# Ten resident units instead of six ahead of each block's first tile in the fourth layer of a four-layer forward and backward pass

## The chip, the cores and the metric

The kernel runs on one core of one Trainium2 chip. The metric is the device time of one execution in microseconds, the median of several runs. TensorE is called PE (its weight loads PEld), VectorE DVE, ScalarE ACT, GpSimd POOL and SyncE SP.

## What is computed

A decode step of four layers and its gradients. The layers alternate between attention over a window of a key/value cache and an MLP with a Mish activation, and both kinds use the same weights twice:

```python
x = x + _A_ref(_layernorm(x), A_k_cache, A_v_cache, A_wq, A_wo)   # layer 1
x = x + _B_ref(_layernorm(x), B_w1, B_b1, B_w2)                   # layer 2
x = x + _A_ref(_layernorm(x), A_k_cache, A_v_cache, A_wq, A_wo)   # layer 3
x = x + _B_ref(_layernorm(x), B_w1, B_b1, B_w2)                   # layer 4
```

x has one row of 1024. Attention has 32 query heads and 4 key/value heads of 128, caches of 32768 positions of which the last 4096 are used, wq of 1024 x 4096 and wo of 4096 x 1024. The MLP has w1 of 1024 x 3584 and w2 of 3584 x 1024. All is bfloat16. Outputs are x and the gradients of x, both caches (4 x 32768 x 128 each), wq, wo, w1, b1 and w2. The caches' gradients are zero outside the window of 4096, so most of the bytes that the kernel writes are zeros.

## The kernel before

Every matrix product has a single row of x on one side, so each weight is read once by PE per use, and the weights have to be on the chip in two orientations: one for the forward product, the other for the backward one. The kernel keeps wq, K, V and wo in SBUF and turns them in place. A *unit* is a piece of 128 x 1024 of one of them; turning it is eight PE transposes of 128 x 128 into a PSUM tile `tp` (lines L258 and L282) and one copy back by ACT (L231) or DVE (L229). Units wait in a list sorted by the tensor's rank (wo, V, K, wq), and `fill(n)` turns the next n at the place in the program where it stands. `fill_kind(kind)` turns all that are left up to that kind, directly ahead of the product that needs them. Three PSUM tiles are shared by everything named `tp`, `op` or `dhp`.

The fourth layer (`mlp_B4`) needs w1 in both orientations. It works in four blocks of w1's columns: three of 1024 and one of 512. A block is loaded as four tiles of 512 KB (the last block as two) into the four buffers of ring `r4`, which lie in the K tensor, so that a block takes all of them. Per block come, in this order: `fwd` (for each tile first `fill(FT4[b][i])`, then the tile's matmuls), `fill(FB4[b][0])`, a selection and the Mish, `turn` (the tile's own transposes), `fill(FB4[b][1])`, `bwd`, and the release of the buffers by `rel`. `rel` calls `pump`, which issues the next loads in the queue (L182 for weights, L190 for K) as far as buffers are free. Then `zeros(ZB4[b])` issues that many transfers of zeros of 512 KB to the caches' gradients (L151, or L149 once the source is the smaller one).

All these transfers stand in SP's one queue in program order. A load whose buffer is not free holds up what stands behind it, and a transfer is held back until the eighth before it has landed.

Behind the fourth layer come the backward passes: layer 3 (`attn_bwd`, with its own lists of fills and zeros, `F_` and `Z_`; its last product `R<-wq` comes after `fill_kind("wq")`), layer 2 (`mlp_B2_bwd`: 14 tiles of w2 through `w2_pass`, then 16 of w1; six buffers of ring `rb` at first, which come free when layer 3 has used K), and layer 1. From there on `run_jobs` makes the weights' gradients as outer products (matmuls with two rows, copied out by `ev_out` at L890 on DVE and L893 on ACT) and writes them out (L965, L978, L996, L1001, L1097). The last zeros are issued among the first of these jobs: the third entry of `add("w2", ...)` says how many.

Of the kernel before, what the change touches and what calls it, by code (L numbers as in the profile page):

```python
# [21 lines left out]
def kernel(  # L22
# [65 lines left out]
    sB, sA, zlo, zt = misc[:, 0:1024], misc[:, 1024:2048], misc[:, 2048:3072], misc[:, 1024:3072]  # L88
# [654 lines left out]
    def attn_bwd(g_col, g_bf, l, sv, last, nxt, F_, Z_, step):  # L743
        fill_kind("wo")
        big = two_banks()
        for d in range(TD):
            for n in range(8):
                mm(big[n // 4][32 * (n % 4):32 * (n % 4) + 32, :].rearrange("p (h x) -> p h x", h=4),
                   bc(g_bf[:, d:d + 1]), wo[:, 4 * n:4 * n + 4, d * P:(d + 1) * P], d == 0, d == TD - 1, tile_position=(0, 32 * (n % 4)))
        if last:  # L750
            p_t, ds_t = sB, wo[:, 1, :]
            wo_dead()
            nc.gpsimd.dma_start(wo[:, 0, :], p3_d[:])
        else:
            p_t, ds_t = sv["p"], sA
        zeros(Z_[0])
        acc = one_tile("acc", HQ)
        j_cols(big, acc, 8, F_[0], True)
        do32 = wk("do32", HQ)
        nc.vector.tensor_copy(pad[:, :, 0:8], acc[:].rearrange("p (g h) -> p g h", g=G))  # L760
        nc.vector.tensor_copy(do32[:], acc[:])
        pr = jkf[:, 0:P]
        nc.vector.tensor_mul(pr[:].rearrange("p (c h) -> p c h", c=NC), do32[:, None, :].to_broadcast([P, NC, HQ]),
                             sv["o32"][:, None, :].to_broadcast([P, NC, HQ]))
        nc.gpsimd.tensor_copy(dos[:, LI[l], :], do32[:])
        step(0)
        fill(F_[1])
        fill_kind("V")
        big = two_banks()
        scores(big, Vf, False)  # L770
        sps = sm_tile(P, 1)
        mm(sps[:], pr[:], one[:], True, True)
        sd = wk("sd", 1)
        nc.vector.tensor_copy(sd[:], sps[:])
        zeros(Z_[1])
        for h in range(2):
            nc.vector.scalar_tensor_tensor(out=ds_t[:, h * 512:(h + 1) * 512], in0=big[h][:], scalar=sd[:, 0:1],
                                           in1=p_t[:, h * 512:(h + 1) * 512], op0=ALU.subtract, op1=ALU.mult)
        sv["p"], sv["ds"] = p_t, ds_t
        if not last:  # L780
            nc.gpsimd.dma_start(p3_d[:], sB)
            nc.gpsimd.dma_start(sB, p1_d[:])
            sv["p"] = wo[:, 0, :]
        step(1)
        fill(F_[2])
        to_keys(ds_t)
        fill_kind("K")
        qacc = one_tile("acc", HQ)
        step(2)
        keys_mm(K[:], fold, qacc, F_[3])  # L790
        if not last:
            rings["rb"] += range(2, 8)
            pump()
        nc.scalar.activation(dqpair[:, LI[l], :], qacc[:], ACT.Copy, scale=scale)
        zeros(Z_[2])
        step(3)
        fill_kind("wq")
        R = one_tile("R", 512)
        for h in range(HQ):
            for hf in range(2):  # L800
                g = 2 * hf + h % 2
                mm(R[32 * g:32 * g + 32, :].rearrange("p (t d) -> p t d", t=4), bc(dqpair[:, LI[l], h:h + 1]),
                   wq[:, 4 * hf:4 * hf + 4, h * P:(h + 1) * P], h < 2, h >= HQ - 2, tile_position=(0, 32 * g))
            if h % 4 == 3 and h < 31:
                step(4)
        y = d_cols(R, hook=lambda: step(5))
        tt = wk("xx", 2 * TD)
        nc.vector.tensor_copy(tt[:, 0:TD], y[:])
        return ln_bwd(tt, sv, g_col, nxt, hook=lambda: step(6))
# [62 lines left out]
    row_sp = {k: wo2[1 + i].rearrange("p (s x) -> p s x", s=2) for i, k in enumerate(("w2", "w1", "wo", "wq"))}  # L872
# [96 lines left out]
    def pair_half(R, c0, out_v, lhs_of, i):  # L969
        cs = [c0, c0 + 1]  # L970
        if i == 0:
            held_st[c0] = {c: stage() for c in cs}
        sts = held_st[c0]
        quad(R, [(*lhs_of(c, tt), slice(i * 512, (i + 1) * 512), sts[c][:, tt * 1024 + i * 512:tt * 1024 + (i + 1) * 512])
                 for c in cs for tt in range(2)])
        if i == 1:
            for c in cs:
                nc.sync.dma_start(out_v[c], sts[c].rearrange("p (t d) -> p t d", t=2))  # L978
# [45 lines left out]
    w2_out = out_8.rearrange("(c p t) d -> c p t d", p=P, t=2)  # L1024
# [3 lines left out]
    def wo_dead():  # L1028
        for sp in spreads:
            nc.gpsimd.memset(sp, 0.0)  # L1030
        w2_sp.append(rows_spread(apair, "blocks"))
        w2_sp.append(rows_spread(gpair[:, 2:4, :], "rep"))

        def rows(name, side, src, how):
            return lambda: rows_spread(src, how), lambda got: rows_turn(row_sp[name], side, got, how)

        def lay(out, src, k):
            return lambda: row_spread(src, k), lambda got: out.append(row_layout(got, k))

        def small_add():  # L1040
            db1 = kt([P, 2, NW2], BF16, "db1")
            nc.vector.tensor_add(db1[:], dh_l[0][:].rearrange("p (c t) -> p t c", t=2), dh_l[1][:].rearrange("p (c t) -> p t c", t=2))
            return db1

        def small(db1):
            col_out(x4_bf_l[0][:], TD, out_0[0, 0, :], 4)
            col_out(g0_l[0], TD, out_1[0, 0, :], 5)
            db_row = kp[0:NW2, 0:2, :].rearrange("c t x -> c (t x)").rearrange("c (p t) -> c p t", t=2)
            for t in range(2):
                dbps = ptile()  # L1050
                nc.tensor.transpose(dbps[0:NW2, 0:P], db1[:, t, :], ident_bf[:])
                nc.vector.tensor_copy(db_row[:, :, t], dbps[0:NW2, 0:P])
            nc.gpsimd.dma_start(out_7.rearrange("(c x) -> c x", x=2 * P), db_row.rearrange("c p t -> c (p t)"))

        prep = {("w2", 1): [rows("w1", 0, npair[:, 2:4, :], "rep")], ("w2", 2): [rows("w1", 1, hpair, "pieces")],
                ("w2", 4): [lay(dos_r, dos[:, 0, :], 0)], ("w2", 5): [lay(dos_r, dos[:, 1, :], 1)], ("w1", 1): [(small_add, small)],
                ("w1", 4): [lay(qs_r, qs[:, 0, :], 2)], ("w1", 5): [lay(qs_r, qs[:, 1, :], 3)],
                ("w1", 8): [rows("wo", 0, opair, "twos")], ("w1", 10): [rows("wo", 1, gpair[:, 0:2, :], "rep")],
                ("w1", 12): [rows("wq", 0, npair[:, 0:2, :], "rep")], ("w1", 14): [rows("wq", 1, dqpair, "heads")]}

        after = []

        def add(kind, n, f, z=0):
            jobs.append((True, f, z))
            while after:
                jobs.append((False, after.pop(0), 0))
            for pre, post in prep.get((kind, n), []):
                got = []
                jobs.append((False, lambda pre=pre, got=got: got.append(pre()), 0))
                after.append(lambda post=post, got=got: post(got[0]))  # L1070

        for n in range(NW2 // 2):
            add("w2a", n, lambda c=2 * n: pair_half(row_sp["w2"], c, w2_out, w2_lhs, 0))
            add("w2", n, lambda c=2 * n: pair_half(row_sp["w2"], c, w2_out, w2_lhs, 1), 1)
        for n in range(16):
            add("w1", n, lambda t=n // 2, hf=n % 2: w1_job(t, hf))
            add("kv", n, lambda n=n: kv_step(n))
        for n in range(HQ // 8):
            add("wo", n, lambda c=4 * n: tall_jobs(row_sp["wo"], range(c, c + 4), wo_out, wo_lhs))
            for i in range(4):  # L1080
                add("wq", n, lambda t=2 * n + i // 2, hf=i % 2: wq_job(t, hf))
# [29 lines left out]
        elif i > 2:  # L1111
            run_jobs(1 if i == 4 else 2)

    ZB4 = [11, 11, 10, 8]
    FT4 = [(0, 0, 0, 0), (6, 2, 2, 2), (6, 2, 2, 2), (8, 3)]
    FB4 = [(1, 0), (1, 0), (1, 0), (1, 2)]

    pump()
    x1, sA1 = attn_fwd(x0, "A1", True, sA, [0] * 6, [0] * 4)
    x2, sB2, da4 = mlp_B2_fwd(x1)  # L1120
    x3, sA3 = attn_fwd(x2, "A3", False, sB, [3, 2, 8, 2, 2, 2], [8, 4, 14])
    tt, sB4 = mlp_B4(x3, da4)
    g3, g3b, _ = ln_bwd(tt, sB4, gcol, "A3", nfill=2)
    g2, g2b, _ = attn_bwd(g3, g3b, "A3", sA3, False, "B2", [4, 3, 5, 2], [5, 1, 5], lambda i: None)
    (g1, g1b, _), x4_bf = mlp_B2_bwd(g2, g2b, sB2, x3)
    zeros(4)
    g0, g0b, _ = attn_bwd(g1, g1b, "A1", sA1, True, "X0", [0] * 4, [0, 0, 0], out_step)
# [39 lines left out]
```

## Time and profile before

| | |
|---|---|
| median of 3 runs | 441.53 us (439.03 to 441.63) |
| the profiled execution's own time | 439.71 us |
| its span | 437.9 us, 9216 instructions |
| PE busy | 322.9 us (74%) |
| DVE busy | 234.0 us (53%) |
| ACT busy | 219.2 us (50%) |
| DMA | 169.98 MB, mean 388 GB/s |
| mean granted PE clock | 0.756 |

One execution is profiled, and its times are microseconds from the start of its span. Beside the span, some 1.8 us belong to the execution's time. The page cuts the span into 40 slices of 10.95 us and gives, for each, the busy share of the engines and of the DMA engines in tenths, the granted PE clock in tenths of full speed, and the GB/s moved. A timeline's row gives the start, the length, the engine, the source line, what is written and read, a count, and in brackets the idle time ahead of it and what ended it.

### The profile page before, as it was taken

The page shows a single profiled execution, that of the slowest core. Times are in us where ns is not written, and L with a number is a line of the kernel's source. Part 1 is how long each engine was busy: PE and PEld are TensorE (multiplying, and loading weights), DVE is VectorE, ACT ScalarE, POOL GpSimd, SP SyncE. Part 2 cuts the span into 40 slices and gives each one's busy share as a digit, 9 for nine tenths or more (in the row PEclk, how much of TensorE's full clock was granted, in tenths as well). Part 3 has the DMA queues.
Part 4 walks back from the last instruction along what each step waited for, and adds up shares of the span by engine and source line. Part 5 has one row for each costly group of instructions (what it writes and reads, how often), then busy time and mean ns, then how long its engine had stood idle before and what let it go on. Part 6 is the DMA issues. An engine that isn't in the chain of part 4 may idle for free.

```text
span 437.9 us, 9216 instructions
## 1 busy us (share of the span) xinstructions
PE 322.9 (74%) x3732; PEld 189.0 (43%) x3732; DVE 234.0 (53%) x532; ACT 219.2 (50%) x335; POOL 15.4 (4%) x54
## 2 busy tenths in 40 slices
PE   3475746477788878588789749767889799999830
PEld 1164315355365666477567427755423123321100
DVE  2035102088364456255565548664266999899940
ACT  1036000046273456356445236464467689899950
POOL 2000000000000000000000000000400020000000
PEclk9999555569898999889999877686875555555555
DMA  8999999999999999998999998999999999999995
GB/s 334 422 420 416 412 409 388 392 378 359 392 414 405 418 328 392 398 416 265 413 410 404 380 413 286 377 370 352 409 423 418 419 414 412 403 402 411 410 412 229
DMA packets 50215, 169.98 MB, mean 388 GB/s; under 512 B 4832, under 2 KB 5884, under 8 KB 46076
## 3 DMA queue, kind: packets, MB, share of 16 engines
q1 hardware_dynamic: 49696, 168.32, 98.2%
q0 software_dynamic: 416, 1.06, 0.6%
q8 instruction: 29, 0.48, 0.4%
q14 instruction: 14, 0.11, 0.1%
q10 hardware_dynamic: 60, 0.01, 0.0%
HBM read 70.27 MB, written 99.10 MB: 387 GB/s over the span
## 4 chain that ended last, share of the span: by engine, by line
PE 18%; DMA 17%; ACT 8%; DVE 4%; issue 2%; SPq 1%; ACTq 0%; DVEq 0%
DMA out_dram<-misc 8%; DMA K<-in_B_w_dram 7%; PE op L238 4%; ACT wo L893 4%; PE R L238 3%; ACT wq L893 2%; PE acc L238 2%; DMA out_dram<-wo 2%; PE sm L238 2%; PE tp L258 2%; ACT K L231 2%; PE lo L238 2%; PE hi L238 1%; PE tp L924 1%; DVE wo L890 1%
## 5 line engine op out<-in xcount | busy, mean ns | idle before, releaser
L231 ACT COPY K<-tp 128x1024 bf16<-128x1024 bf16 x59 | 57.9, 1015 | 22.7 <-PE tp L258 22.1
L258 PE MATMUL tp<-ident_bf,K 128*128 128x128 bf16 x656 | 52.7, 239 | 8.4 <-ACT K L231 3.4
L238 PE MATMUL op<-wo 2*128 2x512 bf16 (+2 forms) x123 | 52.0, 559 | 5.0 <-ACT wo L893 2.7
L231 ACT COPY wo<-tp 128x1024 bf16<-128x1024 bf16 x33 | 33.5, 1023 | 36.3 <-PE tp L258 33.6
L258 PEld LDWEIGHTS <-K 128*128 128x128 bf16 x656 | 44.3, 108 | 16.0 <-issue 11.4
L238 PEld LDWEIGHTS <-wo 128*128 128x128 bf16 (+2 forms) x590 | 24.3, 101 | 62.2 <-issue 53.3
L893 ACT CAST wo<-op 128x512 bf16<-128x512 f32 (+1 forms) x51 | 31.4, 631 | 8.0 <-PE hi L238 2.2
L590 DVE CUSTOM_DVE_ANT_0 K<-K,kp 128x1024 bf16<-128x1024 bf16 (+1 forms) x22 | 24.6, 1127 | 12.5 <-PE R L238 8.8
L258 PE MATMUL tp<-ident_bf,wo 128*128 128x128 bf16 x336 | 26.4, 235 | 0.3 <-ACT wo L231 0.3
L229 DVE COPY jk<-R 128x512 f32<-128x512 f32 (+1 forms) x11 | 7.3, 665 | 34.3 <-PE R L238 34.3
L258 PEld LDWEIGHTS <-wo 128*128 128x128 bf16 x336 | 21.5, 106 | 7.7 <-issue 7.6
L238 PE MATMUL acc<-wo 2*128 2x512 bf16 (+1 forms) x41 | 24.1, 588 | 0.2 <-DVE V L890 0.2
L238 PE MATMUL lo<-wo 2*128 2x512 bf16 x41 | 24.1, 588 | 0.0
L238 PE MATMUL hi<-wo 2*128 2x512 bf16 x41 | 24.0, 586 | 0.0
L229 DVE COPY wo<-tp 128x1024 bf16<-128x1024 bf16 x19 | 12.8, 688 | 16.8 <-PE tp L258 16.8
L238 PE MATMUL sm<-wo 2*128 2x512 bf16 (+1 forms) x33 | 19.8, 600 | 1.3 <-DVE cols L378 1.3
L231 ACT CAST jk<-hi 128x512 bf16<-128x512 f32 x4 | 2.6, 659 | 35.9 <-PE hi L238 35.9
L229 DVE COPY K<-tp 128x1024 bf16<-128x1024 bf16 x23 | 15.6, 689 | 9.1 <-PE tp L258 9.0
L890 DVE CAST wo<-op 128x512 bf16<-128x512 f32 (+1 forms) x32 | 18.4, 598 | 3.7 <-DMA out_dram<-wo 2.3
L238 PE MATMUL R<-wo 2*128 2x512 bf16 (+1 forms) x33 | 19.6, 593 | 0.6 <-DVE wo L890 0.4
L231 ACT COPY wq<-tp 128x1024 bf16<-128x1024 bf16 x14 | 14.1, 1014 | 11.2 <-PE tp L258 8.4
L229 DVE CAST jk<-lo 128x512 bf16<-128x512 f32 x4 | 2.8, 712 | 30.3 <-PE lo L238 30.3
(295 smaller groups left out, 643.0 us busy)
## 6 DMA issues: line engine op xcount, KB each, us to landing
out_dram<-misc SPq DMA_DIRECT2D x97, 512.0 KB, 10.3
out_dram<-wo SPq DMA_DIRECT2D x39, 512.0 KB, 9.5
K<-in_B_w_dram SPq DMA_DIRECT2D x28, 512.0 KB, 10.0
K<-in_A_k_cache_dram SPq DMA_DIRECT2D x9, 1024.0 KB, 15.6
wq<-in_A_wq_dram SPq DMA_DIRECT2D x8, 1024.0 KB, 10.1
out_dram<-wq SPq DMA_DIRECT2D x8, 1024.0 KB, 12.6
K<-in_B_w_dram SPq DMA_DIRECT2D x16, 448.0 KB, 5.8
out_dram<-wo SPq DMA_DIRECT2D x16, 448.0 KB, 7.8
```

What stands on the lines that cost most here:

```text
L229: return nc.vector.tensor_copy(out_ap, in_ap)
L231: return nc.scalar.copy(out_ap, in_ap)
L238: return nc.tensor.matmul(out_ap, lhsT=lhsT, rhs=rhs, start=start, stop=stop, skip_group_check=True, **kw)
L258: nc.tensor.transpose(ps[:, b * P:(b + 1) * P], ap, ident_bf[:])
L590: return nc.vector.tensor_tensor_reduce(out=w, in0=w, in1=vec, scale=1.0, scalar=0.0, op0=ALU.mult, op1=ALU.add, accum_out=acc_col)
L890: nc.vector.tensor_copy(out_ap, in_ap)
L893: nc.scalar.copy(out_ap, in_ap)
L924: nc.tensor.transpose(ps[:, j * P:(j + 1) * P], spread_t[:, j, :], ident_bf[:])
```

## The change

In blocks 1, 2 and 3 (counted from 0) of the fourth layer, ten units instead of six (eight in block 3) are turned ahead of the block's first tile; block 3 turns two instead of three ahead of its second. That makes 50 units turned in the layer instead of 41. The layers behind it turn as many as their lists say, and what is left for `fill_kind("wq")` shrinks accordingly. The zeros are divided anew: two more in the forward pass of layer 3, one more each behind blocks 0 and 1, two fewer behind block 2, one fewer behind block 3, one and two fewer in the backward pass of layer 3, and one more at two of the w2 jobs near the end. Their total is the same.

```diff
--- before.py
+++ after.py
@@ -1071,7 +1071,7 @@
 
         for n in range(NW2 // 2):
             add("w2a", n, lambda c=2 * n: pair_half(row_sp["w2"], c, w2_out, w2_lhs, 0))
-            add("w2", n, lambda c=2 * n: pair_half(row_sp["w2"], c, w2_out, w2_lhs, 1), 1)
+            add("w2", n, lambda c=2 * n: pair_half(row_sp["w2"], c, w2_out, w2_lhs, 1), 2 if n in (2, 4) else 1)
         for n in range(16):
             add("w1", n, lambda t=n // 2, hf=n % 2: w1_job(t, hf))
             add("kv", n, lambda n=n: kv_step(n))
@@ -1111,17 +1111,17 @@
         elif i > 2:
             run_jobs(1 if i == 4 else 2)
 
-    ZB4 = [11, 11, 10, 8]
-    FT4 = [(0, 0, 0, 0), (6, 2, 2, 2), (6, 2, 2, 2), (8, 3)]
+    ZB4 = [12, 12, 8, 7]
+    FT4 = [(0, 0, 0, 0), (10, 2, 2, 2), (10, 2, 2, 2), (10, 2)]
     FB4 = [(1, 0), (1, 0), (1, 0), (1, 2)]
 
     pump()
     x1, sA1 = attn_fwd(x0, "A1", True, sA, [0] * 6, [0] * 4)
     x2, sB2, da4 = mlp_B2_fwd(x1)
-    x3, sA3 = attn_fwd(x2, "A3", False, sB, [3, 2, 8, 2, 2, 2], [8, 4, 14])
+    x3, sA3 = attn_fwd(x2, "A3", False, sB, [3, 2, 8, 2, 2, 2], [8, 4, 16])
     tt, sB4 = mlp_B4(x3, da4)
     g3, g3b, _ = ln_bwd(tt, sB4, gcol, "A3", nfill=2)
-    g2, g2b, _ = attn_bwd(g3, g3b, "A3", sA3, False, "B2", [4, 3, 5, 2], [5, 1, 5], lambda i: None)
+    g2, g2b, _ = attn_bwd(g3, g3b, "A3", sA3, False, "B2", [4, 3, 5, 2], [4, 1, 3], lambda i: None)
     (g1, g1b, _), x4_bf = mlp_B2_bwd(g2, g2b, sB2, x3)
     zeros(4)
     g0, g0b, _ = attn_bwd(g1, g1b, "A1", sA1, True, "X0", [0] * 4, [0, 0, 0], out_step)
```

## Prediction

> **What bounds the kernel now.** I read the page's slices first, then the chain of waits, then the stretches around the change.
>
> ```profile
> PEclk9999555569898999889999877686875555555555
> DMA  8999999999999999998999998999999999999995
> GB/s 334 422 420 416 412 409 388 392 378 359 392 414 405 418 328 392 398 416 265 413 410 404 380 413 286 377 370 352 409 423 418 419 414 412 403 402 411 410 412 229
> ...
> 318.00:426.00 108.00, 92.74 (x518) 26.17 (x514) 90.85 (x171) 89.94 (x178) 4.25 (x17) 0.52 1.02 412
> 421.20:438.00 16.80, 0.00 (x0) 0.00 (x0) 0.05 (x1) 0.46 (x1) 0.00 (x0) 0.50 0.71 290
> ```
>
> The DMA engines are busy in every slice at a little over 400 GB/s. The stretches have us, then PE, PEld, DVE, ACT and POOL busy, granted clock, DMA share, GB/s. In the tail (318 to 426) DMA share is 1.02, and from 421.2 it still writes with no engine working. So the end is set by DMA: the bytes are the same in both kernels, and time can only come from stretches where the transfers ran dry or slowly. The low slices are 15 and 19 (around the edit), 25 and 28.
>
> ```profile
> 157.00:160.00 3.00, 2.86 (x61) 2.63 (x62) 1.11 (x3) 0.78 (x1) 0.00 (x0) 1.00 0.61 179
> ...
> 199.00:202.00 3.00, 2.79 (x63) 2.46 (x53) 0.69 (x1) 1.60 (x2) 0.00 (x0) 1.00 0.47 144
> ...
> 150.98 0.33 SPq L151 DMA_DIRECT2D out_dram<-misc  x1
> 158.15 2.02 SPq L182 DMA_DIRECT2D K<-in_B_w_dram  x4
> 160.22 11.95 SPq L151 DMA_DIRECT2D out_dram<-misc  x11
> 171.84 0.33 SPq L151 DMA_DIRECT2D out_dram<-misc  x1
> 177.07 2.35 SPq L182 DMA_DIRECT2D K<-in_B_w_dram  x4
> 191.47 0.33 SPq L151 DMA_DIRECT2D out_dram<-misc  x1
> 199.79 1.83 SPq L182 DMA_DIRECT2D K<-in_B_w_dram  x2
> 202.21 0.43 SPq L151 DMA_DIRECT2D out_dram<-misc  x1
> ```
>
> The last eight are SP's issues (start, length, count; those at 150.98, 171.84 and 191.47 are the last zeros ahead of a block's loads, 202.21 the first behind the K load). A block's weights of layer four (4 × 512 KB, L182) can be loaded only when the block before has given its buffers back, so the zeros (L151) issued behind the loads are all that DMA has until then. At 157 and at 199 they ran out: 179 and 144 GB/s.
>
> **The change part by part.** SP's order of zeros becomes, at the places 18, 11, 11, 10, 14, 5 of before: 20, 12, 12, 8, 12, 3. Through the second 12 the sum is 64 in both; then two fewer, and two more in the tail's w2 jobs. A zero is 512 KB, 1.25 us at the 418 to 423 GB/s of slices 30 and 31.
>
> Landing is issue plus the median that the list of DMA issues gives for a stretch with one issue:
>
> ```profile
> out_dram<-misc SPq DMA_DIRECT2D x1, 512.0 KB, 10.0
> K<-in_B_w_dram SPq DMA_DIRECT2D x1, 512.0 KB, 4.4
> out_dram<-misc SPq DMA_DIRECT2D x1, 512.0 KB, 10.7
> K<-in_B_w_dram SPq DMA_DIRECT2D x1, 512.0 KB, 4.6
> out_dram<-misc SPq DMA_DIRECT2D x1, 512.0 KB, 9.3
> ```
>
> These are the zero at 150.98 (the same line answers for 191.47), the load at 158.15, the zero at 171.84, the load at 199.79 and the zero at 202.21. They landed at 161.0 (201.5), 162.6, 182.5, 204.4 and 211.5. On a fed queue a load follows its predecessor by 1.3 us (182.5 to the tile at 183.85, next fence); on a dry one it takes 4.4 to 4.6 from its issue.
>
> Block 1, DMA. Two more zeros land until 163.5, so loads issued at 158.15 find no gap: 164.8, 166.1, 167.4, 168.6 for the four tiles. The 18 zeros' gap is closed; what is late is the tiles.
>
> ```profile
> 158.12 2.01 PE L258 MATMUL tp<-ident_bf,wo 128*128 128x128 bf16 x32
> 160.29 1.05 PE L258 MATMUL tp<-ident_bf,wo 128*128 128x128 bf16 x16 [0.16 <-ACT wo L231]
> 162.62 0.40 PE L238 MATMUL hi<-K,npair 128*32 128x512 bf16 x4 [1.28 <-DMA K<-in_B_w_dram]
> ...
> 167.57 0.40 PE L238 MATMUL hi<-K,npair 128*32 128x512 bf16 x4 [0.66 <-DMA K<-in_B_w_dram]
> ...
> 183.85 0.62 PE L238 MATMUL lo<-K,npair 128*32 128x512 bf16 x4 [3.60 <-DMA K<-in_B_w_dram]
> 184.40 1.89 PE L258 MATMUL tp<-ident_bf,wo 128*128 128x128 bf16 x16
> ...
> 206.30 0.40 PE L238 MATMUL hi<-K,npair 128*32 128x512 bf16 x4
> ```
>
> Block 1, PE. Six units (48 transposes) take 158.12 to 161.34, 0.535 us each, evacuations by ACT and DVE included; ten take until 163.5. That is before the new first tile (164.8): the four extra units cost nothing, covered by a wait that grew. Behind the waiting PE stand only the block's own sums, and ACT and DVE copy the same units out meanwhile. If the tile came as early as before, they would cost 163.5 - 162.6 = 0.9. Fourth tile at PE: 164.8 plus three steps of 1.4 (four matmuls, two units) = 168.9, against 167.57. The block ends 1.3 later, about 178.4.
>
> Block 2. Before, 11 zeros took 167.6 to 182.5, 1.36 each; 12 at 1.25 to 1.36 end at 183.6 to 184.9, I take 184.3, the rates of the two blocks' zeros lying between. Tiles: 185.6 to 189.5. Ten units run 178.4 to 183.7, then PE waits 1.9 us where it waited 3.6. Fourth tile at PE 189.8 at full clock, 191 if the clock halves again (184.40: 16 transposes 1.89 instead of 1.07). The block ends at 199.1 to 200.4 (before 199.79).
>
> Block 3. Twelve zeros land until 189.5 + 15.0 = 204.5; the loads, issued by 200.4, are there in time, so DMA does not run dry. From the last zero before (201.5) to the first zero behind the K load (211.5) went 10.0 us for 2.5 MB, a start on an empty queue included. Without the start it is between 6.5 (five units at 1.3) and 9.0 (all as slow as before). I take 8.3, nearer the slow end, as slice 19 holds slow transfers besides the empty 3 us: 212.8. PE: the second tile lands at 208.1 instead of 206.3, so block 3 ends 1.8 late.
>
> ```profile
> 234.16 5.36 PE L258 MATMUL tp<-ident_bf,wq 128*128 128x128 bf16 x80
> 239.45 3.64 PE L238 MATMUL R<-wq,dqpair 128*32 128x512 bf16 x64
> ...
> 234.20:239.40 5.20, 5.15 (x81) 4.61 (x81) 3.57 (x6) 3.38 (x5) 0.00 (x0) 1.00 1.05 403
> ...
> 215.52 11.98 DMA out_dram<-misc
> ...
> 241.21 10.48 DMA K<-in_B_w_dram
> ...
> 251.76 10.24 DMA K<-in_B_w_dram
> ```
>
> Third layer, PE. Ten units (80 transposes) stood before wq's product; counting what is left in the list, one stays, not none. Nine of 0.535 are 4.8 us. With 1.8 late, the product starts 3.0 earlier, and so does the first w2 step of the block behind, 247.76 to 244.7.
>
> Third layer, DMA, in 512 KB units along the chain of waits (the last three rows; start, length). From 211.5 to 227.5, 12 units in 16.0 us; now 10: 226.1. From there to the load that landed at 251.7, 17 units in 24.2, 1.42 each; now 15: 247.4. From there to the seventh w2 tile at 262.0, 8 units in 10.3; now 6: 255.1. So that tile, for which PE waits 6.28 us, comes 6.9 us earlier (6.2 to 8.7 by block 3's bounds). Can it be issued then? Its buffer is released by the first w2 step, 250.8 before, 247.8 now; plus 4.4 is 252.2: yes. Without the nine units gone it would be 257.0, so their removal is worth 1.9 of the 6.9, not 4.8.
>
> The rest moves with it, as nothing there is edited. Two zeros return in the tail: 2 × 512 KB at 412 GB/s, 2.55 us, on the path because DMA is the path there. **Sum: -6.9 + 2.55 = -4.35** on the profiled execution's 439.71, that is 435.4, or 0.990. The runs' median is 441.53, so 437.2.
>
> ```profile
> 247.76 0.42 PE L238 MATMUL R<-K,apair 128*32 128x512 bf16 x4 [0.22 <-DMA K<-in_B_w_dram]
> ...
> 250.46 0.40 PE L238 MATMUL acc<-gpair,K 128*128 128x1 bf16 x8
> ...
> 255.42 0.35 PE L238 MATMUL acc<-gpair,K 128*128 128x1 bf16 x8
> 262.05 0.62 PE L238 MATMUL R<-K,apair 128*32 128x512 bf16 x4 [6.28 <-DMA K<-in_B_w_dram]
> 263.75 0.62 PE L238 MATMUL R<-K,apair 128*32 128x512 bf16 x4
> ...
> 293.29 1.04 PE L258 MATMUL tp<-ident_bf,K 128*128 128x128 bf16 x8 [1.61 <-DMA K<-in_B_w_dram]
> ```
>
> The rows are the w2 steps on PE: the first, the end of the first one's buffer use, the end of the sixth, the seventh and eighth. The wait left for the seventh tile is 255.1 minus (255.4 to 255.8, moved by 3.0: 252.4), 2.7 us. At 262 a step takes 1.7 us at half clock. A wait of 1.61 at 293.29 was followed by eight transposes in 1.04, twice the 0.535 of a unit, so I leave the half clock in behind the 2.7 too. If it stays full, four steps save some 0.4 each, 1.6 us.
> [...]
>
> **The rivals.**
> *Tail on ACT and DVE.* Both are busy 90 of 108 us in the tail. Were they its bound, the two zeros would be free: -6.9, 434.6 on the runs' scale. Against it: DMA works 16 us after their end.
> *The gain is eaten before the tail.* Between 262 and 318 PE and DMA hand over tile by tile, and the clock is 0.6 to 0.8 in slices 24 to 30. If one fall more, or a longer one, costs 1.5 to 3, or block 3's loads stay at 9.0 and more, -1.5 to -2.9 is left: about 439.3, no change. For it: the clock's fall hangs on a fine balance of waits. Against: such falls are paid for already.
> *Half clock under long runs of transposes; slower.* If ten units in a row let the clock halve, a unit costs 0.94 (184.40). Block 1's ten end at 167.5, its fourth tile at 175.0, 7.5 late; the loads of block 2, issued at 184.5, meet a queue dry from 184.3. Block 2 then ends 10.9 late, DMA dry from 207.8; block 3 ends 16.3 late, minus 4.8 is 11.5. The seventh w2 tile can be issued at 262.3 and lands at 266.7: +4.7, with the two zeros +7.2, 448.7. It decides once the units outlast the zeros, about 2 us more per block than now. Against it: the 80 transposes at 234.2 ran with the clock at 1.00.
> [...]
> *The change does not do what it says.* If the second gap stays open because block 2 ends later than 202, only the first is won: about -1.9, 439.6.
>
> **How the numbers follow.** Forecast 0.58, ACT and DVE 0.12, eaten 0.19, second gap 0.04, half clock 0.07. 1% (4.4 us) is about what a measurement of this kernel can tell from no change; the runs shown spread 0.6%. The forecast's own range is -2.5 to -6.5, its centre almost on the bound, so half of it counts as faster (0.31), the rest as same (0.27); of those 0.02 go over to faster for a clock that stays full. Faster: 0.31 + 0.02 + 0.12 = 0.45. Same: 0.25 + 0.19 + 0.04 = 0.48. Slower: 0.07. The range 433.0 to 442.0 takes in the forecast, ACT and DVE, both no-change cases and the runs' scatter; it leaves out the half clock.
>
> **What would show it.** Right: no stretch near 157 or 199 under 300 GB/s; PE waits about 1.2, 1.9 and 0.5 to 1.7 us for the first tiles of blocks 1, 2, 3; 8 instead of 80 transposes ahead of wq's product; the seventh w2 tile near 255 and the tail 6 to 7 us earlier; DMA still writing 12 us and more after the last evacuation. Wrong: a clock of 0.50 while ten units run, a dry queue behind the 12 zeros, or a seventh w2 tile that waits for its buffer instead of the queue.

## The result, and the profile after

The changed kernel takes 437.32 us (median of 22 runs, 433.81 to 441.79) against 439.51 us of the kernel before (22 runs, 436.84 to 442.19): a ratio of 0.9943, interval 0.992 to 0.9966. Two more comparisons gave 0.9965 (0.9939 to 0.9992) and 0.9951 (0.9914 to 0.9988). The kernel before against itself gave 0.9971 (0.9945 to 0.9997) and 0.9995 (0.9954 to 1.0036), so a single ratio carries some 0.3% of chance. The mean of the three ratios is 0.9953: a gain of about 0.5%, 2.1 us, half of the 4.35 us of the sum. Set against the 0.9983 that the unchanged kernel shows on the mean, it is 0.3%, 1.3 us; a gain is likely, its size is not settled. That the forecast time of 437.2 was met is luck: more runs put the kernel before at 439.5 instead of 441.5, and these 2 us are about what the gain fell short by.

The page of the changed kernel, the slices (granted PE clock, busy tenths of DMA, GB/s):

```profile
span 435.1 us, 9216 instructions
...
PEclk9999655569689889989999789855955555555555
DMA  8999999999999989999999999999999999999994
GB/s 332 425 420 416 410 409 390 383 376 365 410 414 403 416 332 375 413 413 385 386 410 401 387 368 312 413 311 421 415 415 418 421 409 407 402 404 412 411 415 203
```

Slice 19, 265 GB/s before, has 385. Slice 15 has 332, before 328: the first hole is still there. (A hole is a stretch in which the transfers have run dry: the first lies ahead of block 1's loads, the second ahead of block 3's.) The stretches of the changed kernel around both holes, and the ten units of block 1 (us, busy time of PE, PEld, DVE, ACT, POOL, clock, DMA share, GB/s):

```profile
157.00:160.00 3.00, 2.25 (x43) 1.83 (x44) 1.86 (x3) 2.27 (x3) 0.00 (x0) 1.00 0.97 391
159.50:162.50 3.00, 2.81 (x61) 2.57 (x62) 1.11 (x3) 0.72 (x1) 0.00 (x0) 1.00 0.47 141
160.70:165.90 5.20, 4.88 (x81) 4.59 (x80) 3.36 (x5) 3.23 (x4) 0.00 (x0) 1.00 0.81 277
199.00:202.00 3.00, 2.33 (x51) 1.81 (x47) 1.13 (x2) 1.95 (x2) 0.00 (x0) 1.00 1.02 412
199.00:202.00 3.00, 2.33 (x49) 1.87 (x49) 1.30 (x3) 1.95 (x2) 0.00 (x0) 1.00 1.04 422
```

(The fourth row is the same stretch in the changed kernel's third profile.) At 199 DMA is fed. At 159.5 it is not: 141 GB/s. PE's timeline of the changed kernel (start, length, what, count, idle time before and who ended it) shows why, and what the ten units met; the last three rows are SP's issues of the loads of blocks 0 and 1 and of the w2 loads from the seventh on:

```profile
160.67 2.01 PE L258 MATMUL tp<-ident_bf,wo 128*128 128x128 bf16 x32
162.84 2.00 PE L258 MATMUL tp<-ident_bf,wo 128*128 128x128 bf16 x32 [0.16 <-ACT wo L231]
164.99 1.05 PE L258 MATMUL tp<-ident_bf,wo 128*128 128x128 bf16 x16 [0.16 <-ACT wo L231]
165.98 0.40 PE L238 MATMUL hi<-K,npair 128*32 128x512 bf16 x4
...
187.25 0.62 PE L238 MATMUL lo<-K,npair 128*32 128x512 bf16 x4 [2.66 <-DMA K<-in_B_w_dram]
187.80 1.89 PE L258 MATMUL tp<-ident_bf,V 128*128 128x128 bf16 x16
...
208.88 0.40 PE L238 MATMUL hi<-K,npair 128*32 128x512 bf16 x4 [1.15 <-DMA K<-in_B_w_dram]
...
237.93 0.61 PE L258 MATMUL tp<-ident_bf,wq 128*128 128x128 bf16 x8
238.47 3.64 PE L238 MATMUL R<-wq,dqpair 128*32 128x512 bf16 x64
...
246.90 0.62 PE L238 MATMUL R<-K,apair 128*32 128x512 bf16 x4
...
249.79 0.40 PE L238 MATMUL acc<-gpair,K 128*128 128x1 bf16 x8
...
257.34 0.40 PE L238 MATMUL R<-K,apair 128*32 128x512 bf16 x4 [1.84 <-DMA K<-in_B_w_dram]
257.68 0.62 PE L258 MATMUL tp<-ident_bf,K 128*128 128x128 bf16 x8
...
259.09 1.04 PE L258 MATMUL tp<-ident_bf,K 128*128 128x128 bf16 x8
...
126.69 2.53 SPq L182 DMA_DIRECT2D K<-in_B_w_dram  x4
160.71 2.02 SPq L182 DMA_DIRECT2D K<-in_B_w_dram  x4
250.26 8.61 SPq L182 DMA_DIRECT2D K<-in_B_w_dram  x6
```

Block 0 ended, and block 1's units began, at 160.7, not at 158.1. The 20 zeros had run out by then, as the 18 had before. Part of what follows is as forecast: PE's waits ahead of blocks 2 and 3 are 2.66 and 1.15 us, and eight transposes stand ahead of wq's product. But PE comes little earlier: wq's product starts at 238.5 (239.5 before, 3.0 earlier forecast), the first w2 step at 246.9 (247.8 before, 244.7 forecast). The load of the seventh w2 tile therefore waited for its buffer: the first step releases it at 250.2, and SP issues the load at 250.3. The tile is used at 257.3 (262.0 before, 255.1 forecast), and PE's wait for it fell from 6.28 to 1.84 us.

The tail starts at 314.2 instead of 319.9 (first `op` product). The means of the three profiles that each kernel has (the experiments below) hold less chance than these two profiles:

| means of three profiles, us | before | after | change | forecast |
|---|---|---|---|---|
| start of wq's product | 239.2 | 239.4 | +0.2 | -3.0 |
| seventh w2 step | 261.1 | 257.4 | -3.7 | -6.9 |
| start of the tail | 318.7 | 314.0 | -4.7 | -6.9 |
| tail, to the end of the span | 117.5 | 120.1 | +2.6 | +2.55 |
| span | 436.1 | 434.0 | -2.1 | -4.35 |

The two zeros cost in the tail what was forecast; what is missing was lost ahead of it.

### The profile page after: what moved, and what is told of

It is laid out like the page before. It is cut to its first block, busy times and chain, and to the rows that moved or that the text cites. A ratio compares the mean times of both kernels' runs of the same rounds, so it can differ in the third digit from the quotient of the medians.

```text
span 435.1 us, 9216 instructions
## 1 busy us (share of the span) xinstructions
PE 323.7 (74%) x3732; PEld 190.5 (44%) x3732; DVE 234.7 (54%) x532; ACT 219.4 (50%) x335; POOL 15.4 (4%) x54
## 4 chain that ended last, share of the span: by engine, by line
PE 21%; DMA 15%; ACT 8%; DVE 5%; issue 2%; ACTq 0%; SPq 0%; DVEq 0%
DMA K<-in_B_w_dram 6%; PE R L238 5%; DMA out_dram<-misc 5%; DMA out_dram<-wo 4%; PE tp L258 4%; ACT wo L893 4%; PE op L238 3%; PE acc L238 3%; ACT wq L893 2%; PE sm L238 2%; PE lo L238 2%; PE hi L238 1%; PE tp L924 1%; ACT K L231 1%; DVE wo L890 1%
## 5 line engine op out<-in xcount | busy, mean ns | idle before, releaser
L231 ACT COPY K<-tp 128x1024 bf16<-128x1024 bf16 x60 | 58.9, 1016 | 20.3 <-PE tp L258 18.6
L258 PE MATMUL tp<-ident_bf,K 128*128 128x128 bf16 x656 | 55.6, 247 | 8.4 <-DMA K<-in_B_w_dram 3.6
L258 PEld LDWEIGHTS <-K 128*128 128x128 bf16 x656 | 47.1, 113 | 15.4 <-issue 10.1
L258 PE MATMUL tp<-ident_bf,wo 128*128 128x128 bf16 x336 | 25.2, 230 | 0.6 <-ACT wo L231 0.5
L231 ACT COPY wq<-tp 128x1024 bf16<-128x1024 bf16 x13 | 13.0, 1018 | 11.2 <-PE tp L258 8.4
L238 PE MATMUL R<-wo,operm 128*32 128x512 bf16 x128 | 11.4, 492 | 9.1 <-DMA wo<-in_A_wo_dram 8.8
```

The lines of the kernel that those rows point to most:

```text
L231: return nc.scalar.copy(out_ap, in_ap)
L238: return nc.tensor.matmul(out_ap, lhsT=lhsT, rhs=rhs, start=start, stop=stop, skip_group_check=True, **kw)
L258: nc.tensor.transpose(ps[:, b * P:(b + 1) * P], ap, ident_bf[:])
```

## The experiments

**Both kernels again.** Their profiles tell how far one profile can be trusted.

> The changed kernel once more, for a second profile and as the yardstick of the three beside it. Theory: DMA sets the end, and the first gap (ahead of block 1's loads) was closed only in executions whose block 0 ends on time; in the changed kernel's first profile PE ran at half clock from 149.5 to 156.3 and block 0 ended at 160.7 instead of 158.2. The clock's place is chance, so this profile may end block 0 anywhere from 158 to 161; where it ends before 159, no stretch near 160 has under 300 GB/s, and the seventh w2 tile comes by 255.5. Time 435 to 438.5, 0.992 to 0.997 of before. Rival: the two zeros more are themselves what ends block 0 late (loads of block 0 slowed by them), then block 0 ends at 160 or later again and the first gap is open again.

> The changed kernel a third time, beside the kernel before on the same chip. So far 0.9943 and 0.9965 of before, and the kernel before against itself 0.9971, so a shift of 0.3% stands for nothing. Theory (emptier time on DMA: two profiles each give 5.5 and 4.1 us of it before, 3.8 and 1.7 after): about 2 us faster, ratio 0.993 to 0.998; block 3's loads meet no dry queue (nothing under 200 GB/s in 198 to 206), while a dry stretch near 160 may or may not stand. Rival (no gain at all, both first ratios chance): 0.998 to 1.003.

> The kernel before once more, for a second profile. In its first profile block 0 ended at 158.2 and the zeros ahead of block 1's loads ran out for little; the three later profiles of kernels with the same program up to there ended block 0 at 159.4 to 161.1. Theory (the first profile was an early one; the changed kernel gains by emptier time on DMA, and the span is that empty time plus a fixed 432): block 0 ends at 159.4 or later, the first gap is 2 to 3 us, the second about 2, ratio to before 1.000 within 0.004. Rival (before really ends block 0 early, and the changed kernel ends it late): 158.2 again.

> The kernel before a third time. Theory: ratio to itself 1.000 within 0.003; a dry stretch of 1 to 2.5 us near 199 to 201 again, since 11 zeros run out before block 2's end, and one near 158 of 1 to 2.5. Rival (the second gap is chance too): no stretch near 200 under 250 GB/s.

Measured: 437.69, 436.25, 438.43 and 437.57 us, with the ratios above; all four lie in their ranges. On the end of block 0 the theory of before_again missed and its rival's number came true: 158.4, where 159.4 or later was expected, and 158.0 in the third profile. In the changed kernel's two profiles it was 160.0 and 158.9. Here are the two stretches with the holes, 150 to 175 and 198 to 222, three profiles of the kernel before, then three of the changed one:

```profile
150.00:175.00 25.00, 19.85 (x298) 16.86 (x299) 14.37 (x47) 15.77 (x19) 0.00 (x0) 1.00 0.97 367
198.00:222.00 24.00, 20.13 (x323) 15.70 (x321) 12.97 (x39) 11.88 (x15) 0.00 (x0) 1.00 0.93 347
150.00:175.00 25.00, 20.34 (x302) 16.96 (x300) 14.74 (x47) 16.26 (x19) 0.00 (x0) 1.00 0.96 366
198.00:222.00 24.00, 20.21 (x332) 16.02 (x331) 12.68 (x39) 12.18 (x14) 0.00 (x0) 1.00 0.97 366
150.00:175.00 25.00, 20.16 (x299) 16.89 (x300) 14.39 (x47) 16.35 (x19) 0.00 (x0) 1.00 0.96 369
198.00:222.00 24.00, 20.26 (x296) 15.73 (x294) 12.52 (x37) 12.04 (x14) 0.00 (x0) 0.93 1.01 384
...
150.00:175.00 25.00, 23.07 (x319) 19.50 (x310) 15.29 (x45) 15.24 (x18) 0.00 (x0) 0.87 0.95 362
198.00:222.00 24.00, 19.03 (x297) 15.33 (x298) 13.67 (x41) 13.33 (x15) 0.00 (x0) 1.00 1.02 389
150.00:175.00 25.00, 21.68 (x316) 17.88 (x309) 14.99 (x44) 14.93 (x18) 0.00 (x0) 0.95 0.98 380
198.00:222.00 24.00, 18.41 (x284) 14.92 (x285) 13.42 (x40) 13.04 (x15) 0.00 (x0) 1.00 1.03 391
150.00:175.00 25.00, 20.72 (x289) 17.76 (x286) 13.70 (x37) 13.31 (x16) 0.00 (x0) 0.91 1.00 384
198.00:222.00 24.00, 18.16 (x278) 14.75 (x279) 13.54 (x40) 12.93 (x15) 0.00 (x0) 0.99 1.03 400
```

The last column, GB/s, is what counts: in a kernel whose end is set by DMA (the changed kernel's tail, 314.2 to 418.9, moved 412 GB/s at a DMA share of 1.02), more bytes by a given moment are time. Means of three profiles each (those of 175 to 198, 222 to 255 and 255 to 300 from the same view):

| stretch | before | after | MB more | at 412 GB/s |
|---|---|---|---|---|
| 150 to 175 | 367 | 375 | 0.20 | 0.5 us |
| 175 to 198 | 408 | 403 | -0.12 | -0.3 us |
| 198 to 222 | 366 | 393 | 0.66 | 1.6 us |
| 222 to 255 | 395 | 389 | -0.22 | -0.5 us |
| 255 to 300 | 353 | 362 | 0.41 | 1.0 us |

The sum is 2.3 us; the spans of the six profiles differ by 2.1, as the runs do. Three more profiles have the changed kernel's program up to 222 (the fewer zeros, the dummies and the five zeros below): 352, 389 and 391 GB/s in the first stretch, 374, 386 and 349 in the third. With them the first hole gives 0.5 us and the second 0.9. So the holes differ from execution to execution by as much as the change closes, and the table's rows are means of few profiles with a wide scatter. The second hole was there in all three of before, but in the third it had shrunk to one microsecond under 250 GB/s (204 at 199 to 200), so the rival of before_third is only just out. And it can open in the changed program too: with five zeros ahead of w2, 201 to 203 had 129 GB/s behind the 12 zeros.

**The tail.** Four zeros less among the w2 jobs:

```diff
+    leave = [4]
     def run_jobs(n):
...
             f()
+            for _ in range(min(z, leave[0])):
+                zero_jobs.pop(0)
+                leave[0] -= 1
+                z -= 1
             zeros(z)
```

> The changed kernel with four transfers of zeros (512 KB each) left out among the tail's w2 jobs, so that this part of the caches' gradients is not written. It takes 4 x 1.27 = 5.1 us of DMA time out of the tail and nothing else. Theory (DMA sets the end): -4.5 to -5.5 us against the changed kernel, ratio to before 0.982 to 0.987. Rival (ACT and DVE, which copy the products out, set the tail's length): 0 to -1.5 us, ratio 0.991 to 0.996.

Measured: 432.39 us, 0.9854 (0.9817 to 0.9891), 4.3 us under the changed kernel by the ratios (0.9951 for it), 4.9 by the medians. The rival is out: ACT and DVE, busy 90 of 105 us there, do not set the tail's length; the bytes do. Their copies themselves ended earlier, 100.0 us behind the tail's start instead of 104.7 (this run's profile and the changed kernel's first).

**The nine units ahead of wq's product.** Their PE time is put back:

```diff
         fill_kind("wq")
+        if not last:
+            for _ in range(9):
+                ps = ptile()
+                for b in range(8):
+                    nc.tensor.transpose(ps[:, b * P:(b + 1) * P], wq[:, 0, b * P:(b + 1) * P], ident_bf[:])
```

> The changed kernel with nine groups of eight extra transposes on PE, whose results are not used and not copied, directly ahead of the third layer's wq product: PE's share of the nine units comes back there and nothing else. Theory (the seventh w2 tile's load waits for a buffer that PE frees, and with three zeros behind the first six loads DMA then runs dry): the product starts 4.8 us later, the seventh tile is issued near 255 and lands near 260 instead of 257, DMA is empty 2 to 4 us more between 245 and 300; +2 to +3.5 us against the changed kernel, ratio to before 0.999 to 1.004. Rival (PE has slack there, since it waits for that tile anyway): 0 to +1 us, ratio 0.994 to 0.998.

Measured: 438.52 us, 1.0002 (0.9975 to 1.0029): 2.2 us over the changed kernel (0.9951 for it), as the theory said, and near the 1.9 that the prediction gave this part. The dummies took 4.2 us, SP issued the seventh load at 253.8 instead of 250.3, and DMA had run out: 102 GB/s from 252 to 255 (PE and SP of this run, then its stretch; the changed kernel's first profile moved 393 there):

```profile
237.86 4.18 PE L802 MATMUL tp<-ident_bf,wq 128*128 128x128 bf16 x72
258.93 0.40 PE L238 MATMUL R<-K,apair 128*32 128x512 bf16 x4
253.76 8.02 SPq L182 DMA_DIRECT2D K<-in_B_w_dram  x7
222.00:255.00 33.00, 29.38 (x445) 21.59 (x433) 15.51 (x32) 10.10 (x12) 1.45 (x3) 0.90 0.96 364
```

The seventh step, at 258.9, no longer waits for its tile. DMA waits for PE instead.

**Units alone, zeros alone.**

```diff
 fills_only = the kernel before with
+    FT4 = [(0, 0, 0, 0), (10, 2, 2, 2), (10, 2, 2, 2), (10, 2)]
 zeros_only = the changed kernel with
+    FT4 = [(0, 0, 0, 0), (6, 2, 2, 2), (6, 2, 2, 2), (8, 3)]
```

> Ten units ahead with the old division of the zeros. Theory: the first gap stays open (18 zeros), but block 2's wait of 3.6 us shrinks to about 1.3 us and its half clock goes, so block 2 ends some 2.4 us earlier and the second gap, 199 to 202, is nearly shut by that alone. The nine units gone ahead of wq's product let the seventh w2 tile be issued in time. -2 to -3 us against before, ratio 0.993 to 0.996: as much as the whole change measured. Rival (the zeros are what closes gaps): 0.998 to 1.001.

> The new division of the zeros with the old units ahead (6, 6 and 8, ten units left for wq's product). Theory (DMA sets the end): the first gap is filled as in the changed kernel; PE waits some 3.5 us for block 1's first tile and over 4 us for block 2's, both times into half clock, so blocks 1 and 2 end 1 to 2 us later each, but DMA still has zeros to write when block 3's loads are issued. The seventh w2 tile's buffer comes free 4.8 us later than in the changed kernel, at about 254, so the tile lands at 258 instead of 255 to 257. Against the changed kernel +1 to +3 us; ratio to before 0.996 to 1.002. Rival (units are free wherever they stand, zeros do it all): as the changed kernel within 1 us, 0.992 to 0.997.

Measured: units alone 437.69 us, 0.9984 (0.9953 to 1.0015); zeros alone 444.06 us, 1.0124 (1.0089 to 1.0159). Both theories missed; units alone lie in their rival's range, zeros alone above both ranges. Zeros alone:

```profile
187.66 0.62 PE L238 MATMUL lo<-K,npair 128*32 128x512 bf16 x4 [4.35 <-DMA K<-in_B_w_dram]
262.77 0.40 PE L238 MATMUL R<-K,apair 128*32 128x512 bf16 x4
242.71 2.72 SPq L149 DMA_DIRECT2D out_dram<-misc  x3
257.60 12.40 SPq L182 DMA_DIRECT2D K<-in_B_w_dram  x10
255.00:300.00 45.00, 36.05 (x525) 28.69 (x524) 33.51 (x65) 29.02 (x31) 0.00 (x0) 0.80 0.88 314
```

PE waits 4.35 us for block 2 and has ten units left ahead of wq's product, so the seventh load is issued at 257.6; but only three zeros stand behind the six loads before it. From 254 to 259 DMA is all but empty (36 GB/s), and from 255 to 300 it moves 314 GB/s instead of the 358 of the changed kernel's first profile: 2.0 MB, 4.8 us. My expectation counted only the later tile and not how long DMA stays thin behind it. The third-layer zeros may be given to the tail only if PE comes early, which the units do.

Units alone:

```profile
184.94 0.40 PE L238 MATMUL lo<-K,npair 128*32 128x512 bf16 x4 [1.62 <-DMA K<-in_B_w_dram]
261.54 0.62 PE L238 MATMUL R<-K,apair 128*32 128x512 bf16 x4 [6.45 <-DMA K<-in_B_w_dram]
185.00:189.00 4.00, 4.00 (x60) 3.01 (x60) 1.98 (x3) 1.40 (x2) 0.00 (x0) 1.00 1.05 405
150.00:175.00 25.00, 22.09 (x329) 18.52 (x322) 15.76 (x48) 16.39 (x19) 0.00 (x0) 0.96 0.92 352
198.00:222.00 24.00, 19.95 (x295) 14.53 (x287) 11.41 (x35) 10.76 (x12) 0.00 (x0) 0.93 1.02 395
255.00:300.00 45.00, 32.57 (x440) 26.54 (x437) 27.79 (x58) 24.97 (x27) 0.00 (x0) 0.72 0.94 345
```

The mechanism expected is there: the wait ahead of block 2 shrinks to 1.62, the clock stays at 1.00 behind it, and the second hole shuts (395 GB/s). So the rival's reason, that zeros close the gaps, is not borne out for this one. But the first hole is as wide as in any profile (352), and with five zeros still ahead of the seventh w2 tile PE stood as long for it as before (6.45 us), and the stretch behind moved 345.

Shown is that the new zeros without the units lose: with the same zeros, the units are worth 6.4 us (444.06 against the 437.69 of after_again, taken on the same chip). Not shown is that the units need the new zeros: on that chip the units alone have the same median, 437.69, and their interval takes in both the changed kernel and no gain at all.

**More zeros ahead of block 1, and another division.**

```diff
 two_more_early, against the changed kernel
-    ... [3, 2, 8, 2, 2, 2], [8, 4, 16])         and   2 if n in (2, 4) else 1
+    ... [3, 2, 8, 2, 2, 2], [8, 4, 18])         and   1
 refit, the same and
-    ZB4 = [12, 12, 8, 7]   ... [4, 1, 3]
+    ZB4 = [11, 11, 8, 8]   ... [5, 1, 3]
 five_ahead_of_w2, against the changed kernel
-    ... [4, 1, 3]                               and   2 if n in (2, 4) else 1
+    ... [4, 1, 5]                               and   1
```

> The changed kernel with the two zeros of the tail's w2 jobs moved to the third layer's forward pass: 22 zeros instead of 20 ahead of block 1's loads. Theory (zeros are worth something only where DMA would run dry, and the first gap is open in most executions): the first gap closes, block 1's tiles come up to 2.5 us later in DMA's queue; -1 to -2.5 us against the changed kernel, ratio to before 0.988 to 0.993. Rival (the first gap is closed with 20 zeros already): the two zeros only change places, block 1's tiles and all behind them come 2.5 us later and the tail is 2.5 us shorter: within 0.7 us of the changed kernel.

> The changed kernel's ten units with another division of the zeros: 22 ahead of block 1's loads, 11 and 11 behind blocks 0 and 1, 8, then 14 and 3, one at each of the tail's w2 jobs. Theory (a zero is worth its time where DMA would run dry, and costs where it delays a tile past PE): the first gap is closed as with 22 zeros, but the loads of blocks 2 and 3 stand behind one zero less each than there, so PE waits under 2 us per block and the wq product starts by 241; two zeros stand in the third layer instead of the tail, so DMA does not run dry ahead of the w2 loads. -0.5 to -2 us against the changed kernel, ratio to before 0.989 to 0.994. Rival (any zero ahead of block 1 just pushes all of PE's chain back): as two_more_early, 0.997 to 1.001.

> The changed kernel with its two zeros of the tail put back where before had them, behind the first six w2 loads (5 instead of 3). Theory (bytes only change places, DMA is fed at both): the seventh w2 tile comes 2.5 us later, near 260, the tail is 2.5 us shorter; within 1 us of the changed kernel, ratio to before 0.993 to 0.999. Rival (the two zeros moved to the tail are what wins, because the w2 steps and their half clock come earlier and shorter): +1.5 to +3 us against the changed kernel, 0.999 to 1.003; second rival (they cost in the tail without winning ahead of it): -1.5 to -2.5.

Measured: 438.18 us, 0.999 (0.9964 to 1.0016); 438.29 us, 0.9987 (0.9964 to 1.0011); 437.46 us, 0.9979 (0.9944 to 1.0013). The first two theories missed, and the times lie in their rivals' ranges. Two more early, in the slowest of its 13 executions (441.83 us) (PE, then the stretch ahead of the w2 loads):

```profile
168.34 0.40 PE L238 MATMUL hi<-K,npair 128*32 128x512 bf16 x4 [3.46 <-DMA K<-in_B_w_dram]
214.22 0.62 PE L238 MATMUL hi<-K,npair 128*32 128x512 bf16 x4 [3.83 <-DMA K<-in_B_w_dram]
222.00:255.00 33.00, 28.31 (x415) 19.89 (x412) 15.43 (x42) 12.01 (x14) 1.45 (x3) 0.91 0.95 343
```

The first hole closes, and the tiles come so late that PE waits 3.46 and 3.83 us and DMA is thin in 222 to 255 (343 GB/s): in this execution the hole has moved. The rival had the number right, but not the reason, for in the changed kernel's first profile the first hole was open. Refit has 390 GB/s in the first stretch and 354 in 198 to 222, since its 11 zeros ran out ahead of block 3 as before's did. Neither is shown to beat the changed kernel. Five zeros ahead of w2 cost 1.2 us against it (0.9979 against 0.9951), inside the intervals: whether the two zeros in the tail win anything stays open. Its expectation, within 1 us and 0.993 to 0.999, is about met.

## Why the prediction was right or wrong

The time was met, the gain was half of the forecast one. The term that was mis-sized is the -6.9 by which the seventh w2 tile, and with it the tail, was to come earlier: it measured -3.7 at the tile and -4.7 at the tail. Two steps under it failed, the first hole and PE's start of wq's product.

- *DMA sets the end*: right; four zeros less took 4.3 to 4.9 us of 5.1 possible.
- *The first hole is closed by two more zeros, 1.9 us* (the price in the last rival, which the prediction does not work out): failed. "Two more zeros land until 163.5, so loads issued at 158.15 find no gap" took 158.15 from one profile. In the ten profiles that are not of the kernel before, block 0 ended at 157.7 to 162.7, and where it ended late the zeros were used up by then. The term measured 0.5 us. The mechanism itself holds: with 20 zeros the stretch 150 to 175 moved 380 to 391 GB/s where block 0 ended at 157.7 to 160.0 (four profiles), and 352 to 362 where it ended at 160.7 to 162.7 (three).
- *Did the two zeros themselves end block 0 late* (the rival of after_again)? No. They stand behind block 0's loads, and from the issue of these loads to the end of block 0 it took 32.4 to 34.1 us in the four profiles with 18 zeros and in the nine with more. What differs is when these loads are issued: 124.0 to 126.1 in the four, 124.9 to 128.6 in the nine, and up to there the programs are the same. Why the executions differ so early is open.
- *The second hole, and the loads behind it, about 1.8 us* (four zeros more, 5.0 us, have landed only 1.3 later; less the 1.9): right in kind, 0.9 to 1.6 measured.
- *Ten units hidden behind a wait*: right ahead of blocks 2 and 3 (2.66 and 1.15 us still waited). In block 1 of the first profile the tile was there when the ten were done (165.98, no wait); in the other two PE waited from the second tile on, 0.24 to 1.25 us for one.
- *PE reaches wq's product 3.0 us earlier* (nine units less, block 3 ends 1.8 late): failed, it came 0.2 later on the mean. Block 0 ended 1.7 later, blocks 1 and 2 3.4 and 3.3 later where 1.3 and about 0 were forecast; that used up the 4.8 us of the nine units.
- *The queue, not the buffer, sets the seventh w2 tile*: failed, and the prediction had named this as a sign of being wrong. Its load was issued as soon as the buffer was free (250.2 and 250.3), while the forecast had the buffer free at 247.8. The tile came earlier all the same, 7.1 us behind its issue instead of 10.3, with three zeros ahead of it in the queue instead of five.
- *The nine units are worth 1.9, not 4.8*: 2.2 measured, but the 1.9 was worked out for a tile held by the queue, so the agreement is partly luck.
- *The half clock ahead of block 2*: in the changed kernel's first profile it fell again (187.80: sixteen transposes 1.89); the prediction allowed for both and priced it as hidden, which it was, by the 12 zeros.
- *Two zeros cost 2.55 in the tail*: right, 2.6 between the means of three profiles.
- *The rivals*: ACT and DVE fell with the four fewer zeros. Half clock under long runs of transposes fell in the changed kernel's own profile: 80 transposes from 160.7 at a clock of 1.00. "The gain is eaten before the tail" came nearest in size, but what ate it was the first hole and a PE that came no earlier, not the clock or block 3's loads.

## What to carry to other kernels

Where transfers set the end, price a change by the bytes moved up to a given moment, hole by hole; here two more zeros won bytes where the queue had run dry (375 GB/s instead of 367 in 150 to 175, means of three profiles), and filler writes won nothing where they delayed a load past the engine that waits for it (two more early: waits of 3.46 and 3.83 us, 343 GB/s in 222 to 255). So filler work on PE and filler writes on DMA have to be looked at together: here the new writes without the new work lost 1.2%, while the new work alone could not be told from the whole change. And a hole read from one profile is not that of the next (three profiles of the kernel before moved 347, 366 and 384 GB/s in 198 to 222, 2.2 us apart at 412 GB/s): take several profiles of the same kernel before a term of the sum rests on one, and measure the unchanged kernel against itself before a gain of 0.5% is believed.

## What the runs showed of the hardware

The granted clock fell to half in or behind short waits of PE in the changed kernel's first profile: with 2.66 us ahead of block 2 (187.80: sixteen transposes 1.89 us; the clock at 0.53 from 187 to 188, at 0.50 from 188 to 190) and 1.84 us ahead of the seventh w2 step (259.09: eight transposes 1.04 us, against 0.62 at 257.68; the clock at 1.00 from 257 to 258, 0.87 from 258 to 259, 0.50 from 259 to 262). It did not fall behind 1.62 us in the kernel with the units alone (1.00 from 185 to 189), though it had fallen with 1.61 us in the kernel before (293.29; 0.69 from 292 to 293, 0.50 from 293 to 296). From the start of that 1.84 us wait to the fall (255.5 to 258.7, the clock at 1.00) PE was busy for 1.22 of 3.2 us. How long a wait has to be for the clock to fall is not shown: 1.61 and 1.62 us went different ways.
